# Retention and two MLPs on one core: Strassen in both products from the second MLP's first block on

## The chip, the cores and the metric

The kernel runs on one core of one Trainium2 chip. The metric is the device time of one execution in microseconds (us), lower is better. The profile splits a core into TensorE (PE, with its weight loads PEld), VectorE (DVE), ScalarE (ACT), GpSimd (POOL) and SyncE (SP); the last two only issue DMAs here.

## The reference, cut to what matters

```python
for t in range(S):                      # B, H, S, D = 4, 8, 768, 64
    state = gamma * state + k[t] (x) v[t]
    y[t] = scale * q[t] @ state
x = y as (B * S, H * D)                 # 3072 tokens x 512
h = x @ w_in;  x = max(0.01 * h, h) @ w_out          # first layer, 512 -> 2048 -> 512
h = max(x @ moe2_w_in, 0);  out = (h * h) @ moe2_w_out   # second layer, same sizes
```

Everything is float32, and the weights reach the chip as float64 words.

## The kernel before

**Blocks.** The 3072 tokens are cut into NB = 3 blocks of TB = 1024 tokens (c = one third of the sequence, for all four batches). A layer runs block by block, first layer first. A float32 product is made of three float32r matmuls, high*high, low*high, high*low (`product` line 470, `emit_out` line 577), so each operand is split into a rounded part (a copy on ACT) and a remainder (a subtraction on DVE).

**Two ways to multiply.** The "in" product of a block (1024 tokens, 512 to 2048) is plain in the first block of the first layer (`emit_plain`, line 535: 384 matmuls of 512 columns) and by Strassen's seven products elsewhere (`emit_in`, line 495: 8 steps q of 42 matmuls, 336). The "out" product (2048 to 512) is plain in the first layer and in block 0 of the second (`emit_out`: 16 parts j, two halves of 512 tokens, 12 matmuls each, 384). Blocks 1 and 2 of the second layer go through `both_block` (line 697), which has Strassen in both: a first stretch with `first_half` and `second_half` (336 matmuls), then seven stages over `STAGES` with the weight combinations of `read_stage` (336 matmuls).

**Weights.** `cast` (line 292) turns a staged tile of 128 x 1024 float64 words into float32: two activations on ACT (L296, L297), a shift, a bit merge and an addition on DVE (L298, L299, L302). `make_in` (line 334) adds and splits the seven combinations of an in-weight and stores them in `wid`; `make_out` (line 372) splits an out-weight and stores it in `wou`. First-layer weights are cast in block 0 (`plain_in`, `make_out`), and combined in block 1 (`make_in`, through `wraw`). Five of the eight second-layer in-weights (`AHEAD`) are cast and combined beside block 2 of the first layer; the other three, and all eight out-weights, in block 0 of the second. `out_combinations` (line 388) makes the four sums of an out-weight that Strassen needs: q = 0, 1 at the end of block 0, q = 2 to 7 beside the first stretch of block 1 (lines 713 to 723).

**Attention.** One pair of heads of one batch and one block is a unit `up`. `load_pair` brings q, k and v; `prep_pair` (line 143) scales q and v on DVE (L148, L154); `scores` (line 172) multiplies k by q into two PSUM banks `sc`, for blocks 1 and 2 both from `ps_h` (three banks, tag "h", which also hold `pa`, `pd`, `pb` of the in product), and masks them on DVE (L193); `values` (line 207) fills bank `y`. `score_next` (line 247) preps and scores one pair in the middle of each step q, `values` follows at the end of the step. Block 0's attention runs before everything (lines 791 to 801), block 1's and block 2's beside the blocks ahead of them.

**Order.** `pin` (line 101) fixes the order on PE, on SP (`load`) and on POOL (`store`) to that of the program text. ACT and DVE are ordered when the program is built, by readiness; `tc.issue_after(mark[0])`, `(mark[1])` puts a helper's ACT and DVE work behind the split marked last (`split_g`, `split_rot`). SP holds all loads, POOL all stores but the last two. Every engine takes its instructions in that order: an instruction that waits holds up those behind it.

Of the kernel before, what the change touches and what calls it, by code (L numbers as in the profile page):

```python
# [9 lines left out]
F32 = mybir.dt.float32  # L10
# [32 lines left out]
AHEAD = {0: 0, 1: 1, 3: 2, 5: 4, 6: 6}  # L43
# [7 lines left out]
def retention_then_two_mlps(  # L51
# [47 lines left out]
    behind = {}  # L99

# [27 lines left out]
    def load_pair(up):  # L128
# [9 lines left out]
        t = [a_p.tile([P, T], F32, tag=f"r{i}", name="r", bufs=2 + i) for i in range(2)]  # L138
# [4 lines left out]
    def prep_pair(up):  # L143
# [3 lines left out]
        qs = a_p.tile([P, 2, P], F32, tag="qs", name="qs", bufs=1)  # L147
# [24 lines left out]
    def scores(up):  # L172
# [67 lines left out]
    n_load, n_prep, n_done = [0], [0], [0]  # L240
# [6 lines left out]
    def score_next(last):  # L247
        n = n_prep[0]
        if n < last:
            loads_to(n + 1)  # L250
            prep_pair(ups[n])
            scores(ups[n])
            n_prep[0] += 1

    def value_to(n):
        while n_done[0] < n:
            values(ups[n_done[0]])
            n_done[0] += 1
            loads_to(n_done[0] + 2)

    def attend(last):

        n = n_prep[0]
        score_next(last)
        value_to(min(n, last))
        loads_to(min(n_done[0] + 3, n_prep[0] + 2))
# [4 lines left out]
    wraw = {}  # L271
# [4 lines left out]
    for q in range(NQ):  # L276
        wraw[q] = dram.tile([P, 1024], F32, name=f"wraw{q}")
    wou = [dram.tile([P, 8 if lay else 4, NQ, 2, 256], F32, name=f"wou{lay}") for lay in range(2)]
    for b in range(NB):
        ydr[b] = dram.tile([P, KB, TB], F32, name=f"ydr{b}")  # L280
    src = (w1, w2)
    stage, n_stage = {}, [0]

    def load_w(lay, q, half):
        if (lay, q, half) in stage:
            return
        n_stage[0] += 1
        pool, bufs = (late["p"], 1) if late and n_stage[0] % 3 == 0 else (w_p, 2)
        t = stage[lay, q, half] = pool.tile([P, 1024], U64, tag="sg", name="sg", bufs=bufs)
        load(out=t, in_=src[lay][q, half])  # L290
# [34 lines left out]
    def plain_in(q):  # L325
        load_w(0, q, 0)
        f = w_p.tile([P, 4, 256], F32, tag="wf", name="wf", bufs=1)
        cast(stage.pop((0, q, 0)), f.rearrange("p n c -> p (n c)"))
# [5 lines left out]
    def make_in(lay, b, q, ahead=False):  # L334
        f = w_p.tile([P, 7, 256], F32, tag="wf", name="wf", bufs=1)
        mid = f[:, 1:5].rearrange("p n c -> p (n c)")
        if lay == 0:
            load(out=mid, in_=wraw[q])
        else:
            load_w(lay, q, 0)  # L340
            cast(stage.pop((lay, q, 0)), mid)
        nc.vector.tensor_tensor(out=f[:, 0], in0=f[:, 3], in1=f[:, 4], op=ALU.subtract)
        nc.vector.tensor_tensor(out=f[:, 4], in0=f[:, 4], in1=f[:, 1], op=ALU.add)
        nc.vector.tensor_tensor(out=f[:, 5], in0=f[:, 1], in1=f[:, 0], op=ALU.subtract)
        nc.vector.tensor_tensor(out=f[:, 6], in0=f[:, 2], in1=f[:, 5], op=ALU.subtract)
        if ahead:
            a = late["p"].tile([P, 2, 4, 256], F32R, tag="ea", name="ea")
            c = late["p"].tile([P, 2, 3, 256], F32R, tag="eb", name="eb")
        else:
            a, c = in_tiles(lay, b, q)  # L350
        pair_up(a, f[:, 3:7])
        pair_up(c, f[:, 0:3])
        store(out=wid[lay, q][:, 0:2048], in_=a.rearrange("p l n c -> p (l n c)").bitcast(F32))
        store(out=wid[lay, q][:, 2048:3584], in_=c.rearrange("p l n c -> p (l n c)").bitcast(F32))
        if not ahead:
            put_in(lay, q, a, c)
# [7 lines left out]
    def get_in(lay, b, q):  # L364
        if lay == 0 and b == 0:
            plain_in(q)
        elif (lay == 0 and b == 1) or (lay == 1 and b == 0 and q not in AHEAD.values()):
            make_in(lay, b, q)
        else:
            read_in(lay, b, q)  # L370

    def make_out(lay, q):
        load_w(lay, q, 1)
        if lay == 0 and 0 < q < NQ - 1:
            f = g_p.tile([P, 2, T], F32, tag=f"t{NQ - 1}", name="of", bufs=1).rearrange("p j c -> p (j c)")
        elif lay and q:
            f = late["p"].tile([P, 1024], F32, tag=("ea", "eb")[q % 2], name="of")
        else:
            f = w_p.tile([P, 1024], F32, tag="wf", name="of", bufs=1)
        cast(stage.pop((lay, q, 1)), f)  # L380
        o = o_p.tile([P, 4, 2, 256], F32R, tag="wo", name="wo", bufs=2)
        pair_up(o.rearrange("p n l c -> p l n c"), f.rearrange("p (n c) -> p n c", n=4))
        put_units(lay, q, 0, o)
        wout[lay, q] = o
        if lay:
            store(out=wraw[q], in_=f)

    def out_combinations(q, f, ta, tb):
        load(out=f, in_=wraw[q])
# [7 lines left out]
        for n, t in ((0, ta), (2, tb)):  # L397
            u = t.bitcast(F32R).rearrange("p (n l c) -> p n l c", n=2, l=2)
            h = f[:, n * 256:(n + 2) * 256].rearrange("p (n c) -> p n c", n=2)
            nc.scalar.copy(u[:, :, 0], h)  # L400
            nc.vector.tensor_tensor(out=u[:, :, 1], in0=h, in1=u[:, :, 0].bitcast(F32), op=ALU.subtract)
            store(
                out=wou[1][:, 4 + n:6 + n, q].rearrange("p n l c -> p n (l c)"),
                in_=t.rearrange("p (n c) -> p n c", n=2),
            )
# [8 lines left out]
    def put_units(lay, q, n, t):  # L414
        store(
            out=wou[lay][:, n:n + 4, q].rearrange("p n l c -> p n (l c)"),
            in_=t.bitcast(F32).rearrange("p n l c -> p n (l c)"),
        )

    def read_out(lay, q, spare=None):  # L420
        if spare:
            o = spare[0].tile([P, 4, 2, 256], F32R, tag=spare[1], name="wo", bufs=spare[2])
        else:
            o = o_p.tile([P, 4, 2, 256], F32R, tag="wo", name="wo", bufs=2)
        load(
            out=o.bitcast(F32).rearrange("p n l c -> p n (l c)"),
            in_=wou[lay][:, 0:4, q].rearrange("p n l c -> p n (l c)"),
        )
        wout[lay, q] = o
# [56 lines left out]
    def act_sbuf(lay, g, on_act):  # L486
        if lay == 0:
            nc.scalar.activation(out=g, in_=g, func=AF.Lrelu)  # L488
        elif on_act:
# [5 lines left out]
    def emit_in(lay, b, q):  # L495
# [13 lines left out]
        nc.vector.tensor_tensor(out=c12, in0=c12, in1=pd, op=ALU.add)  # L509
        act_sbuf(lay, c12, True)  # L510
        yield
        product(lay, b, q, 7, pa, False, True)
        nc.vector.tensor_tensor(out=c22, in0=c22, in1=pa, op=ALU.add)  # L513
        act_sbuf(lay, c22, True)
# [4 lines left out]
        act_sbuf(lay, c11, False)  # L519
# [3 lines left out]
        if lay == 0:  # L523
            nc.scalar.activation(out=g, in_=pa, func=AF.Lrelu)
        else:
            nc.scalar.activation(out=g, in_=pa, func=AF.Relu)
# [470 lines left out]
```

## Time and profile before

| | us |
|---|---|
| median of 3 runs | 1148.55 (1140.07, 1148.55, 1153.57) |
| the profiled execution | 1139.64 |
| its span, first to last instruction | 1137.9 |
| attention of block 0 and first products | 0 to 60.5 |
| first layer: block 0 / 1 / 2 | to 272.1 / 488.4 / 654.1 |
| second layer: block 0 / 1 / 2 | to 823.2 / 979.3 / 1134.1 |

The stage limits are the times at which PE takes up the first `pa` product of the next block in the timeline. Matmuls overlap in the records, so a row's mean of 395 ns is not the pitch; the pitch is a stage's time over its matmuls.

### The profile page before, as it was taken

To read this page: it belongs to the slowest core of one execution; us is meant where nothing else is said; L and a number is where in the kernel's file an instruction comes from. 1 tells how busy PE (TensorE), PEld (TensorE's weight loads), DVE (VectorE), ACT (ScalarE), POOL (GpSimd) and SP (SyncE) were. 2 spreads that over 40 slices of the span, in tenths; PEclk is the share of its full clock that TensorE was granted. 3 is DMA by queue.
4 is the path that set the end of the run, shared out by engine and by line. 5 is a ranking of instruction groups with operands and counts; after the bars stand their busy time and mean duration, and the time that the engine had idled before them with its cause. 6 is when DMAs were issued, how large, how long until landed. Compare 5 with 4: busy or idle time off the path is not lost.

```text
span 1137.9 us, 14882 instructions
## 1 busy us (share of the span) xinstructions
PE 1109.4 (97%) x5690; PEld 879.7 (77%) x5690; DVE 678.1 (60%) x1082; ACT 541.9 (48%) x847; POOL 74.7 (7%) x130
## 2 busy tenths in 40 slices
PE   7899999999999999999999999999999999999998
PEld 5567777777777777788888887788787888888886
DVE  6856564555453535544467567777357877555853
ACT  3635453323433333344455366665256655455542
POOL 0000000001000000010001010111101000000000
PEclk9999999999999999999999999999999999999999
DMA  9556563666556555479788878957869967257571
GB/s 362 222 190 236 204 240 121 225 197 217 186 200 209 200 188 184 158 291 355 265 316 313 325 268 323 389 210 244 305 242 361 366 209 300 87 192 249 192 241 56
DMA packets 75015, 274.14 MB, mean 241 GB/s; under 512 B 6976, under 2 KB 9536, under 8 KB 64704
## 3 DMA queue, kind: packets, MB, share of 16 engines
q1 hardware_dynamic: 57120, 197.81, 49.0%
q0 software_dynamic: 17248, 74.98, 17.2%
q8 instruction: 45, 0.74, 0.3%
q10 hardware_dynamic: 576, 0.40, 0.1%
q14 instruction: 26, 0.21, 0.1%
HBM read 197.66 MB, written 75.50 MB: 240 GB/s over the span
## 4 chain that ended last, share of the span: by engine, by line
PE 86%; DMA 7%; DVE 4%; ACT 2%; issue 1%; ACTq 0%; SPq 0%; DVEq 0%
PE acc L113 41%; PE pa L113 25%; PE pd L113 8%; PE pb L113 5%; DMA wf<-wraw 4%; PE y L113 4%; PE sc L113 3%; DMA wo<-wou 1%; DMA wa<-wid 1%; DMA qt<-qtab 1%; ACT sg L297 1%; ACT wa L322 1%; DVE pm L193 0%; ACT of L296 0%; DVE g L509 0%
## 5 line engine op out<-in xcount | busy, mean ns | idle before, releaser
L113 PE MATMUL acc<-gh,wo 128*128 128x512 f32 x800 | 211.1, 395 | 1.2 <-DMA wo<-wou 1.2
L113 PE MATMUL pa<-xh,wa 128*128 128x512 f32 x576 | 182.6, 398 | 6.3 <-ACT g L483 2.2
L113 PEld LDWEIGHTS acc<-gh,wo 128*128 128x128 f32 x800 | 148.9, 188 | 37.1 <-issue 2.4
L113 PE MATMUL acc<-rot,wu 128*128 128x512 f32 x672 | 157.1, 395 | 0.0
L113 PEld LDWEIGHTS acc<-rot,wu 128*128 128x128 f32 x672 | 126.1, 188 | 30.6
L113 PEld LDWEIGHTS pa<-xh,wa 128*128 128x128 f32 x576 | 106.4, 188 | 33.2 <-ACT g L483 2.6
L113 PE MATMUL pa<-xl,wa 128*128 128x512 f32 x288 | 113.4, 394 | 1.5 <-DVE xl L439 1.5
L113 PE MATMUL acc<-gl,wo 128*128 128x512 f32 x400 | 113.6, 391 | 0.0
L113 PE MATMUL pd<-xh,wa 128*128 128x512 f32 x320 | 99.9, 394 | 0.9 <-ACT g L483 0.9
L113 PE MATMUL pa<-xh,wb 128*128 128x512 f32 x320 | 100.2, 394 | 0.0
L574 DVE TENSOR_TENSOR gl<-g,gh 128x512 fp32r<-128x512 f32 x100 | 67.7, 688 | 49.9 <-PE acc L113 29.5
L113 PEld LDWEIGHTS acc<-gl,wo 128*128 128x128 f32 x400 | 75.1, 188 | 16.6
L113 PE MATMUL acc<-gg,wo 128*128 128x512 f32 x336 | 83.7, 398 | 0.0
L573 ACT CAST gh<-g 128x512 fp32r<-128x512 f32 x100 | 60.5, 619 | 43.6 <-PE acc L113 43.3
L113 PEld LDWEIGHTS acc<-gg,wo 128*128 128x128 f32 x336 | 62.6, 188 | 15.6 <-issue 1.4
L113 PEld LDWEIGHTS pd<-xh,wa 128*128 128x128 f32 x320 | 60.4, 190 | 15.2 <-ACT g L483 2.2
L639 DVE TENSOR_TENSOR rot<-gu,rot 128x512 fp32r<-128x512 f32 x80 | 54.7, 688 | 26.8 <-ACT rot L638 26.5
L113 PEld LDWEIGHTS pa<-xh,wb 128*128 128x128 f32 x320 | 59.2, 188 | 13.7 <-DVE g L513 0.6
L638 ACT CAST rot<-gu 128x512 fp32r<-128x512 f32 x80 | 49.7, 621 | 42.2 <-PE acc L113 36.6
L488 ACT ACTIVATE g<-g 128x512 f32<-128x512 f32 x48 | 30.3, 632 | 82.1 <-DVE g L513 36.0
L113 PEld LDWEIGHTS pa<-xl,wa 128*128 128x128 f32 x288 | 54.3, 189 | 13.5 <-DVE xl L439 1.9
L113 PE MATMUL pd<-xl,wa 128*128 128x512 f32 x160 | 62.7, 392 | 0.0
(117 smaller groups left out, 1573.4 us busy)
## 6 DMA issues: line engine op xcount, KB each, us to landing
wo<-wou SPq DMA_DIRECT2D x40, 1024.0 KB, 7.2
sg<-w SPq DMA_DIRECT2D x32, 1024.0 KB, 8.7
wa<-wid SPq DMA_DIRECT2D x29, 1024.0 KB, 8.6
wu<-wou SPq DMA_DIRECT2D x56, 512.0 KB, 5.2
wb<-wid SPq DMA_DIRECT2D x29, 768.0 KB, 7.0
wou<-wo POOLq DMA_DIRECT2D x16, 1024.0 KB, 5.6
r<-first SPq DMA_DIRECT2D x48, 256.0 KB, 3.5
wid<-wa POOLq DMA_DIRECT2D x11, 1024.0 KB, 4.3
```

The costliest lines, as they stand in the source:

```text
L113: pin(nc.tensor.matmul(**kw))
L297: nc.scalar.activation(out=lo, in_=lo, func=AF.Copy, scale=2.0 ** -29)
L322: nc.scalar.copy(t[:, 0], s)
L488: nc.scalar.activation(out=g, in_=g, func=AF.Lrelu)
L573: mark[0] = nc.scalar.copy(gh, g).ins
L574: mark[1] = nc.vector.tensor_tensor(out=gl, in0=g, in1=gh.bitcast(F32), op=ALU.subtract).ins
L638: mark[0] = nc.scalar.copy(r[:, 0], s).ins
L639: mark[1] = nc.vector.tensor_tensor(out=r[:, 1], in0=s, in1=r[:, 0].bitcast(F32), op=ALU.subtract).ins
```

## The change

Block 0 of the second layer goes through `both_block` as well. Its weights are made earlier. `SOON` lists 12 of the 16 second-layer weights (all in-weights, out-weights q = 4 to 7); each is cast in three pieces of 384, 384 and 256 columns, 20 pieces beside block 0 of the first layer and 16 beside block 1, and stored as plain float32 in `wflt`. The combinations of in-weights `FIRST` (2, 3, 5, 7) are made in eight halves beside block 1 (`make_half`), those of 0 and 1 in SBUF at the end of block 2, those of 4 and 6 inside `both_block(0)` (`units_here`). `make_units` makes all eight units of an out-weight: q = 0 to 3 (`HERE`, cast there from float64) and q = 4 beside block 2, q = 5 to 7 in `both_block(0)`. All these loads are issued by `store`, on POOL's queue. In block 1 of the first layer `make_in` stands earlier in the step. Separately, `prep_pair` runs one pair ahead of `scores`, and in the middle of a step the second `sc` bank is `y` of `ps_a`. `both_block(1)` has no weights to make any more.

```diff
+FIRST = (2, 3, 5, 7)
+HERE = (0, 1, 2, 3)
+SOON = [(q, 0) for q in FIRST + (0, 1, 4, 6)] + [(q, 1) for q in range(NQ) if q not in HERE]
...
-        late["p"] = mid.enter_context(tc.tile_pool(name="late", bufs=1))
+        late["p"] = mid.enter_context(tc.tile_pool(name="late", bufs=1, reuse_waits="tile"))
...
+    @contextmanager
+    def aside():
+        with tc.issue_after(mark[0]), tc.issue_after(mark[1]):
+            yield
...
-        t = [a_p.tile([P, T], F32, tag=f"r{i}", name="r", bufs=2 + i) for i in range(2)]
+        t = [a_p.tile([P, T], F32, tag=f"r{i}", name="r", bufs=3) for i in range(2)]
...
-            sc = [ps_h.tile([P, 512], F32, tag="h", name="sc") for h in range(2)]
+            other = (ps_a, "y") if alone else (ps_h, "h")
+            sc = [p.tile([P, 512], F32, tag=t, name="sc") for p, t in ((ps_h, "h"), other)]
...
+    def prep_to(n):
+        while n_prep[0] < min(n, len(ups)):
+            loads_to(n_prep[0] + 1)
+            prep_pair(ups[n_prep[0]])
+            n_prep[0] += 1
...
+        if last:
+            prep_to(min(n_score[0] + 1, last))
...
+    def load_piece(n):
+        if n < 3 * len(SOON):
+            q, half, c = piece(n)
+            t = stage[n] = a_p.tile([P, 384], U64, tag=f"m{4 - n % 2}", name="st", bufs=1)
+            store(out=t[:, :c.stop - c.start], in_=w2[q, half][:, c])
+
+    def cast_piece(n):
+        q, half, c = piece(n)
+        f = a_p.tile([P, 384], F32, tag="sf", name="sf", bufs=2)[:, :c.stop - c.start]
+        cast(stage.pop(n)[:, :c.stop - c.start], f)
+        store(out=wflt[q, half][:, c], in_=f)
...
+    def combine(f, a, c, x=None):
+        tt = nc.vector.tensor_tensor
+        here = x is None
+        if here:
+            split_low(c, 1, 3, f[:, 2:4])
+            x = f[:, 1:4]
+        split_low(a, 0, 1, f[:, 0:1])
+        tt(out=f[:, 0], in0=f[:, 0], in1=f[:, 1], op=ALU.subtract)
+        tt(out=x[:, 0], in0=f[:, 1], in1=f[:, 2], op=ALU.add)
+        tt(out=x[:, 1], in0=f[:, 2], in1=f[:, 0], op=ALU.subtract)
+        tt(out=x[:, 2], in0=f[:, 3], in1=x[:, 1], op=ALU.subtract)
+        if here:
+            yield
+        split_low(a, 1, 4, x[:, 0:3])
+        if not here:
+            yield
+            split_low(c, 1, 3, f[:, 2:4])
+        split_low(c, 0, 1, f[:, 0:1])
...
+    def make_units(q, f, *to):
+        if q in HERE:
+            t = late["p"].tile([P, 1024], U64, tag="sg", name="sg")
+            store(out=t, in_=w2[q, 1])
+            yield
+            cast(t, f)
+        else:
+            store(out=f, in_=wflt[q, 1])
+        yield
+        h = [f[:, n * 512:n * 512 + 512].rearrange("p (n c) -> p n c", n=2) for n in range(2)]
+        for n in range(2):
+            out_units(q, 2 * n, h[n], to[n])
         yield
...
-            if b == 1:
+            if b == 0 and n < NQ - 1 and n != 5:
...
+                if n in (0, 2, 4):
+                    made = make_units(5 + n // 2, *v[:5])
                     next(made)
+                    if n == 0:
+                        here = [units_here(4, v[5], v[7]), units_here(6, v[6], v[5])]
...
+    def side(n):
+        if n_piece[0] < 3 * len(SOON):
+            next_piece()
+            if n < NQ:
+                next_piece()
...
+        elif n % 2:
+            next_half()
...
+                if b == 1:
+                    side(2 * q)
+                elif 0 < q < 6 and q - 1 in HERE:
+                    with aside():
+                        next(made)
...
+            elif nl and 0 < q < 6:
+                with aside():
+                    next(made)
+                    next(made, None)
+                if q < 5:
+                    made = units_ahead(q)
...
+    for b in range(NB):
+        both_block(b)
```

## Rows read from the trace of the kernel before

**Rows 1.** The page, part 1: busy time and share of the span by engine.

```profile
span 1137.9 us, 14882 instructions
PE 1109.4 (97%) x5690; PEld 879.7 (77%) x5690; DVE 678.1 (60%) x1082; ACT 541.9 (48%) x847; POOL 74.7 (7%) x130
```

**Rows 2.** Busy time by stretch: limits, length, each engine's busy time, clock, DMA.

```profile
core 0: us, PE busy (x) PEld busy (x) DVE busy (x) ACT busy (x) POOL busy (x), PEclk, DMA share, GB/s
0.00:60.50 60.50, 48.05 (x496) 33.75 (x496) 45.52 (x104) 28.23 (x53) 2.15 (x7) 0.97 0.72 274
60.50:200.10 139.60, 137.54 (x760) 107.60 (x760) 78.47 (x116) 68.14 (x90) 9.84 (x15) 0.99 0.56 204
...
272.10:417.00 144.90, 138.11 (x718) 106.33 (x716) 64.52 (x120) 55.82 (x93) 9.06 (x17) 0.99 0.57 202
...
488.40:654.10 165.70, 165.70 (x721) 135.08 (x720) 90.78 (x120) 81.58 (x123) 10.94 (x21) 1.00 0.83 312
654.10:823.20 169.10, 166.97 (x722) 134.64 (x721) 117.56 (x154) 99.97 (x145) 19.50 (x33) 1.00 0.79 290
823.20:979.30 156.10, 154.84 (x673) 125.96 (x672) 113.90 (x182) 87.77 (x147) 13.79 (x22) 1.00 0.75 278
979.30:1134.10 154.80, 154.79 (x673) 125.95 (x671) 88.02 (x135) 74.61 (x127) 3.79 (x7) 1.00 0.53 180
823.20:901.10 77.90, 76.64 (x338) 63.05 (x337) 53.77 (x97) 46.66 (x83) 9.97 (x15) 1.00 0.84 310
979.30:1055.70 76.40, 76.40 (x338) 63.24 (x337) 40.01 (x61) 39.88 (x70) 0.54 (x1) 1.00 0.59 202
277.40:281.90 4.50, 4.50 (x12) 3.27 (x12) 1.93 (x2) 1.99 (x3) 1.07 (x2) 0.62 0.79 316
```

**Rows 3.** Waits of PE: us in total, times, longest.

```profile
PE sc L113 <- DVE g L509: 4.6, 6, 1.4
...
PE sc L113 <- DVE vs L154: 3.1, 5, 1.1
...
PE pa L113 <- ACT g L483: 2.2, 1, 2.2
...
PE pa L113 <- DMA wa<-wid: 1.3, 1, 1.3
```

**Rows 4.** DVE's groups by shape: count, busy us, mean ns, idle before.

```profile
L299 DVE SCALAR_TENSOR_TENSOR wf<-sg,wf 128x1024 uint32<-128x1024 uint32 x16 | 19.5, 1219 | 0.2
...
L298 DVE TENSOR_SCALAR wf<-wf 128x1024 uint32<-128x1024 uint32 x16 | 11.3, 704 | 15.2 <-ACT wf L296 14.9
...
L401 DVE TENSOR_TENSOR of<-of 128x512 fp32r<-128x512 f32 x16 | 10.9, 684 | 1.5 <-ACT of L400 1.5
...
L343 DVE TENSOR_TENSOR wf<-wf 128x256 f32<-128x256 f32 x16 | 6.8, 426 | 0.6
...
L148 DVE TENSOR_TENSOR qs<-r,qt 128x128 f32<-128x128 f32 x16 | 4.6, 284 | 1.7 <-DMA qt<-qtab 1.4 <-PE y L113 0.2
```

**Rows 5.** ACT's groups by shape, the same columns.

```profile
L483 ACT COPY g<-pa 128x512 f32<-128x512 f32 x48 | 28.2, 587 | 40.4 <-PE pa L113 40.4
...
L296 ACT ACTIVATE wf<-sg 128x1024 f32<-128x1024 f32 x16 | 18.2, 1138 | 4.7 <-DMA sg<-w 4.7
L232 ACT COPY xs<-y 128x256 f32<-128x256 f32 x48 | 17.8, 371 | 41.5 <-PE y L113 41.4
```

**Rows 6.** ACT's waits for staged weights: the same in 0 to 270 and overall.

```profile
ACT sg L297 <- DMA sg<-w: 5.6, 5, 2.2
...
ACT wf L296 <- DMA sg<-w: 4.7, 1, 4.7
...
ACT of L296 <- DMA sg<-w: 3.1, 2, 2.0
```

**Rows 7.** DMA issues: queue, count, size, median us from issue to landing.

```profile
sg<-w SPq DMA_DIRECT2D x32, 1024.0 KB, 8.7
...
wou<-wo POOLq DMA_DIRECT2D x16, 1024.0 KB, 5.6
```

**Rows 8.** POOL's issue instructions of line 119: ns min/median/max.

```profile
L119 POOL DMA_DIRECT2D wraw<-wf x8: 554/554/942, 27.5 to 171.1; - x8
```

More of the change, by code (lines that the diff above doesn't have):

```diff
@@ L170, in increment, with scores @@
             )
-    def scores(up):
+    def scores(up, alone):
         u, p = up
@@ L280, in retention_then_two_mlps, with load_w, piece @@
         ydr[b] = dram.tile([P, KB, TB], F32, name=f"ydr{b}")
[L281 to L290, printed above, removed]
+    stage = {}
+    def load_w(q, half):
+        t = stage[q, half] = w_p.tile([P, 1024], U64, tag="sg", name="sg", bufs=2)
+        load(out=t, in_=w1[q, half])
+    def piece(n):
+        k, part = divmod(n, 3)
+        return *SOON[k], slice(384 * part, min(384 * part + 384, 1024))
+    def load_piece(n):
[8 more added lines that the diff above has]
+        store(out=wflt[q, half][:, c], in_=f)
     def cast(s, r):
@@ L332, in plain_in @@
         win[0, q] = a
[L334 to L356, printed above, removed]
@@ new lines, in blocks, with put_wid, make_in @@
+    def blocks(q, half=None):
+        t = wflt[q, 0].rearrange("p (n c) -> p n c", n=4)
+        return t if half is None else t[:, :, half * P:half * P + P]
+    def put_wid(lay, q, t, half=slice(None)):
+        o, m = (0, 8) if t.shape[2] == 4 else (2048, 6)
+        store(
+            out=wid[lay, q][:, o:o + m * 256].rearrange("p (n c) -> p n c", n=m)[:, :, half],
+            in_=t.rearrange("p l n c -> p (l n) c").bitcast(F32),
+        )
+    def make_in(b, q):
+        f = w_p.tile([P, 4, 256], F32, tag="wf", name="wf", bufs=1)
+        load(out=f.rearrange("p n c -> p (n c)"), in_=wraw[q])
+        a, c = in_tiles(0, b, q)
+        for _ in combine(f, a, c):
+            pass
+        put_wid(0, q, a)
+        put_wid(0, q, c)
+        put_in(0, q, a, c)
@@ new lines, in load_half, with make_half @@
+    def load_half(n):
+        if n < 2 * len(FIRST):
+            f = stage[-1, n] = a_p.tile([P, 4, P], F32, tag="sf", name="wf", bufs=2)
+            store(out=f, in_=blocks(FIRST[n // 2], n % 2))
+    def make_half(n):
+        a = a_p.tile([P, 2, 4, P], F32R, tag="m4", name="ma", bufs=1)
+        c = a_p.tile([P, 2, 3, P], F32R, tag="m3", name="mc", bufs=1)
+        f = stage.pop((-1, n))
+        half = slice(n % 2 * P, n % 2 * P + P)
+        for _ in combine(f, a, c):
+            pass
+        put_wid(1, FIRST[n // 2], a, half)
+        put_wid(1, FIRST[n // 2], c, half)
@@ L396, in out_combinations @@
         tt(out=a12, in0=a12, in1=a22, op=ALU.subtract)
[L397 to L405, printed above, removed]
+        for n in range(2):
+            out_units(q, 4 + 2 * n, h[n], to[2 + n])
     def scratch(*tags):
@@ L623, in read_units, with units_here @@
         put_in(1, q, a, c)
+    def units_here(q, f, *x):
+        store(out=f, in_=wflt[q, 0])
+        yield
+        f, *x = (v.rearrange("p (n c) -> p n c", n=4) for v in (f, *x))
+        a, c = unit_tiles()
+        put_in(1, q, a, c)
+        steps = combine(f, a, c, *x)
+        next(steps)
+        if x:
+            put_wid(1, q, a)
+        yield
+        next(steps, None)
+        if not x:
+            put_wid(1, q, a)
+        put_wid(1, q, c)
     def read_stage(n, ks):
@@ L806, in read_x, with put_out, next_piece, next_half @@
         load(out=xs[NB + b], in_=ydr[b])
-    def put_out(lay, b, j, part=(0, 12)):
-        emit_out(lay, b, 0, j, part, j == 0, j == NJ - 1)
+    def put_out(b, j, part=(0, 12)):
+        emit_out(0, b, 0, j, part, j == 0, j == NJ - 1)
+    n_piece, n_half = [0], [0]
+    def next_piece():
+        n = n_piece[0]
+        if n == 0:
+            load_piece(0)
+            load_piece(1)
+        with aside():
+            cast_piece(n)
+        load_piece(n + 2)
+        n_piece[0] += 1
+    def side(n):
[3 more added lines that the diff above has]
+                next_piece()
+            if n_piece[0] == 3 * len(SOON):
+                load_half(0)
+                load_half(1)
+        elif n % 2:
+            next_half()
+    def next_half():
+        with aside():
+            make_half(n_half[0])
+        load_half(n_half[0] + 2)
+        n_half[0] += 1
+    def units_ahead(q):
+        f = late["p"].tile([P, 1024], F32, tag="of", name="of", bufs=2)
+        to = [w_p.tile([P, 2, 1024], F32, tag="sg", name="of", bufs=2) for _ in range(2)]
+        g = make_units(q, f, *(t[:, n] for t in to for n in range(2)))
+        next(g)
+        return g
     def split_late(i):
@@ L936 @@
+    swap_right()
+    for b in range(NB):
+        both_block(b)
 _OUT = ((NB, P, KB, TB), "float32")
```

401 lines of the change are left out of this document (197 added, 204 removed).

## The prediction

> **What bounds the kernel now.** I read the page's busy shares first [rows 1]: PE is busy 1109.4 of 1137.9 us, DVE 60%, ACT 48%. So PE sets the time, and a change pays by taking matmuls away, by closing the 28.5 us in which PE stands, or not at all. The second view is busy time by stretch, cut where PE takes up a new block [rows 2]. The reader is to see two things there. First, block 2 of the second layer is 672 matmuls in 154.8 us with PE busy all of it: 0.2304 us each. Block 2 of the first layer has 720 in 165.7, 0.2301 each, also without a stop. That is the pitch of a covered PE. Block 0 of the second layer has 720 in 169.1; at the pitch that is 165.9, so 3.2 us are stops. Second, the large gaps are elsewhere: 12.4 us in the first 60.5, 2.1 in 60.5 to 200.1, 6.8 in 272.1 to 417. The third view, PE's waits, names them [rows 3]: scores behind DVE's addition L509 (4.6 us, six times), scores behind the scaled v (3.1 us, five times), one product behind ACT's copy (2.2 us).
>
> One stop is dearer than its wait. After that copy, 12 matmuls took 4.5 us at a granted clock of 0.62 [rows 2], so mostly at 1.2 instead of 2.4 GHz, against 2.8 us at the pitch. A stop of 2.2 us costs 3.9.
>
> **The change part by part.**
>
> *Second layer, block 0.* The out product falls from 384 to 336 matmuls, 48 x 0.2304 = 11.1 us. What the block then looks like is seen in block 1 of before, which also makes weights beside its first stretch: 156.1 us, 1.3 above block 2, its one wait being for `wa` from `wid` [rows 2, 3]. The side work on DVE, which is the fuller engine: a `make_units` is 2 x 0.684 for the plain units and 4 x 0.426 + 2 x 0.684 for the sums [rows 4], 1.37 + 3.07; three make 13.3. A `units_here` is splits of 256, 768, 512 and 256 columns (0.43 + 0.95 + 0.68 + 0.43, the 768 set between 512 and 1024) and four sums of 256, 4.19; two make 8.4. Together 21.7 us; block 1 of before had six sums of 3.07, 18.4. Block 2, without side work, has DVE busy 40.0 in 76.4 of its first stretch [rows 2], 5.0 per step of 9.55. Step 3 now gets 3.08 (first part of `units_here`) and 1.37: 9.45 of 9.55; step 4 gets 1.11 + 3.07: 9.18. DVE is full for two steps. I charge 1.0 us for that, so 157.1 instead of 169.1: **-12.0**. Bounds: 154.8 (-14.3) if all is covered, and 154.8 + 21.7 = 176.5 (+7.4) if PE waited for every side instruction.
>
> *Second layer, block 1.* Its six sums go away: 156.1 becomes the 154.8 of block 2, **-1.3** (0 to -1.3).
>
> *Second score bank.* In a step `pa` and `pd` hold two of three `ps_h` banks, so the second `sc` waits until L509 has added `pd`. With `y`, free since the last step's `values`, it does not: **-4.6** (0 to -4.6) [rows 3]. Late next is the mask on DVE, needed only for `values` at the end of the step.
>
> *Scaled q and v ahead.* It can take away the 3.1 us of waits for v, all in the first 60 us. But DVE is busy 45.5 of 60.5 there [rows 2] and does the same work; order alone changes. I take half, **-1.5** (0 to -3.1). The third `r` buffer and the second `qs` cost nothing but space; their loads are the same, issued earlier on SP, where none of the waits on PE comes from.
>
> *Pieces and halves beside the first layer.* A 384-column piece on DVE: shift 0.30 (an estimate, 384/1024 of 0.704 and a start), merge and addition 0.55 each, between 0.426 and 0.684 [rows 4]: 1.41. A 256 one: 0.25 + 2 x 0.43 = 1.10. On ACT 2 x 0.48 and 2 x 0.37, between 0.371 and 0.587 [rows 5]. Two of three are 384 wide, so a mean of 1.31 and 0.89. A half of `make_half`: four sums of 128 columns at 0.284 and splits of 256, 128, 384 and 128: 2.69 on DVE, some 1.35 on ACT. In 60.5 to 200.1 fifteen pieces lift DVE from 78.5 to 98 and ACT from 68 to 82 of 139.6; in 272.1 to 417 sixteen pieces and four halves lift DVE from 64.5 to 96 and ACT from 56 to 75 of 144.9 [rows 2]. That is 70% at most, no more than block 0 of the second layer carried (117.6 of 169.1) with PE busy 99%. Bytes: in the first layer's block 1 a third of 16 weights' 1.5 MB and eight halves of 1.1 MB are 17 MB in 216 us, 82 GB/s on top of 202; 312 GB/s were moved in block 2 without a stop of PE [rows 2]. So capacity hides it all. What may show is order. A cast's first instruction on ACT waits for its load, and behind it stand the copies that free PE's banks. Slack for such a copy: after product 1, PE has product 5 (6 matmuls) and an out part (12), 4.2 us, less the copy's 0.59 [rows 5]: 3.6 us. ACT waited for staged weights up to 4.7 us before [rows 6]. The pieces' loads go to POOL's queue, behind stores that wait for DVE, and in block 1's first four steps two casts stand together twice, so that the next two loads have about 9 us to land; a 1 MB transfer takes 5.6 to 8.7 [rows 7], the pieces being smaller. I charge one stop of the size above: **+3.9**. Bounds: 0, and eight such stops, one for each of those doubles, 31.2.
>
> *Block 2 of the first layer.* Out go five in-weights made ahead (cast 3.14, four sums 1.70, splits 1.22 + 0.95: 7.0 of DVE each), in come four out-weights of cast, eight units and sums (3.14 + 4 x 0.684 + 1.70 = 7.6) and one without cast (4.4): 34.8 for 35.0. In the last stretch two `units_here` add 8.4. The four cast weights are loaded by POOL behind the four stores of the weight before. If each were as late as 4.7 us, PE would see 4.7 - 3.6 = 1.1 of it, 4.4 in all; I take **+1.0** (0 to 4.4).
>
> The moved `make_in` issues the same loads in the same order on SP (wf, r, wo, step after step), and the finer pool release comes where PE has no stop; both at 0, with the bounds of the pieces around them, since they share ACT's order.
>
> Sum: -12.0 - 1.3 - 4.6 - 1.5 + 3.9 + 1.0 = **-14.5**. The profiled execution took 1139.64, so it would take 1125.1. The runs' median is 1148.55, 8.9 above; from it the sum gives 1134.1. A new measurement can fall on either level, so I take the middle, **1129.6**.
>
> *A rule against it.* The issue of a DMA by POOL took 0.55 us, at most 0.94 [rows 8], in a span in which DVE ran 32 shifts of 0.70 us: no issue was held up by as much as one shift. The Trainium skill (SBUF — State Buffer, "Who interferes with whom") says that a DMA issued from GpSimd can seem held up by a DVE operation, because GpSimd is kept from writing its descriptors. By that rule each of the some 56 loads moved from SP to POOL would start up to a shift later; two pieces ahead that moves no term, and it would only make the slower rival below likelier. The trace does not bear it out, and I leave that rival low.
>
> **The rivals.**
>
> *Given back beside the work.* Two more stops of 3.9 in the first layer, and a tenth of the 21.7 us showing in block 0 beyond the 1.0: -14.5 + 7.8 + 2.2 = -4.5, **1140**. For it: DVE is full in two steps, ACT has waited for weights. Against it: block 1 of before lost 1.3 in the same position.
>
> *Late pieces, slower.* In block 1 of the first layer, steps 0 to 3, each pair of casts stops ACT longer than the slack of 3.6 us, from where PE stands and its clock falls: eight stops, 31.2 instead of 3.9, so 1129.6 + 27.3 = **1157**. For it: POOL's queue is in order and holds stores that wait for DVE. Against it: only two casts between load and use need be late for nothing to show, and ACT never waited for a weight after the first layer's block 0 [rows 6].
>
> *Everything covered.* All lower ends: -14.3 - 1.3 - 4.6 - 3.1 = -23.3, **1121**. For it: two blocks of 165.7 and 154.8 without a stop. Against it: the full DVE steps.
>
> *The attention edits do nothing* (DVE is the one that is late): -14.5 + 6.1 = -8.4, 1136; this lies within the forecast's own range, 1121 to 1138.
>
> **How the numbers follow.** Forecast 0.55, given back 0.25, late pieces 0.07, everything covered 0.13. A measurement of this kernel can tell about 1%, 11.5 us, from no change. Faster by more: most of the forecast (0.50), the covered case and a little of the first rival, 0.65. Within: 0.05 and most of "given back", 0.27. Slower: 0.08. The range runs from 1113 (all lower ends from the profiled execution, 1116, and 3 us for the stop at 277 going too) to 1148 (given back, counted from the median: 1144, and one more stop).
>
> **What would show it.** Right: the page has 5642 matmuls; the second layer's three blocks take about 157, 155 and 155 us; no wait of scores behind L509's successor; DVE over 90% in steps 3 and 4 of the new block. Wrong: waits of PE behind ACT's copies with ACT waiting for a DMA of a piece, a granted clock well below 1 in 272 to 420, or a first stretch of the new block over 85 us.

## The result and the profile after

The changed kernel takes 1151.14 us (median of 20 runs, 1148.1 to 1163.49), the kernel before 1144.41 beside it (20 runs): a ratio of 1.006 [1.0033, 1.0087], so slower by 0.6%. The forecast was 1129.6, a gain, and 1151.14 lies outside its range too. Medians are of all runs; ratios leave out the few that were over 1.5% slower than their kernel's fastest, all at a lower granted clock. The profiled execution took 1154.02. The page's first part:

```profile
span 1152.3 us, 15363 instructions
PE 1112.5 (97%) x5642; PEld 879.0 (76%) x5642; DVE 723.8 (63%) x1285; ACT 567.3 (49%) x978; POOL 136.8 (12%) x230
```

48 matmuls fewer than [rows 1], as written, yet PE is busy 3 us longer. Busy time by stretch, cut as [rows 2] (the first limit is where the first out product starts), shows where:

```profile
0.00:87.70 87.70, 68.48 (x550) 48.64 (x551) 57.32 (x119) 36.55 (x62) 3.02 (x9) 0.79 0.68 249
87.70:299.40 211.70, 205.92 (x1190) 159.72 (x1189) 132.17 (x244) 98.82 (x159) 34.57 (x62) 0.97 0.66 229
299.40:516.30 216.90, 207.05 (x1169) 157.66 (x1168) 137.33 (x315) 102.51 (x208) 47.83 (x77) 1.00 0.78 266
516.30:683.70 167.40, 166.41 (x721) 134.93 (x721) 91.07 (x139) 82.71 (x136) 24.56 (x40) 1.00 0.84 309
683.70:838.90 155.20, 155.20 (x673) 125.99 (x672) 117.08 (x186) 91.09 (x155) 18.74 (x31) 1.00 0.76 280
838.90:993.50 154.60, 154.60 (x673) 126.14 (x672) 100.13 (x146) 81.05 (x134) 4.32 (x8) 1.00 0.61 218
993.50:1148.20 154.70, 154.70 (x673) 125.96 (x671) 88.02 (x135) 74.60 (x127) 3.78 (x7) 1.00 0.53 180
```

The first rows of the kernel before, cut at the same places (71.1, and 272.3 where [rows 2] has 272.1):

```profile
0.00:71.10 71.10, 57.56 (x551) 40.82 (x552) 49.77 (x112) 31.20 (x57) 2.87 (x8) 0.95 0.73 273
71.10:272.30 201.20, 200.23 (x1189) 156.13 (x1188) 114.89 (x188) 88.04 (x122) 12.01 (x20) 1.00 0.55 197
272.30:488.40 216.10, 209.31 (x1169) 161.10 (x1168) 102.51 (x190) 78.71 (x130) 11.77 (x23) 0.99 0.57 198
```

The second layer did what was forecast: block 0 fell from 169.1 to 155.2, block 1 from 156.1 to 154.6, with PE busy all of both. That is 15.5 us won. The first layer lost more: the stretch ahead of its out products grew from 71.1 to 87.7, block 0 from 201.2 to 211.7, block 1 from 216.1 to 216.9, block 2 from 165.7 to 167.4, together 29.6. Only 14.5 of the 29.6 are stops of PE. The other 15.1 are a longer busy time for the same matmuls; the largest parts are 10.9 at the start, where the mean clock was 0.79 against 0.95, and 5.7 in block 0, at 0.97 against 1.00. DVE was busy 63% of block 1 and ACT 47%: neither is full. PE's waits name other places than [rows 3]:

```profile
PE y L121 <- DVE state L243: 8.7, 6, 5.2
PE pa L121 <- ACT g L563: 4.6, 2, 2.7
PE sc L121 <- DMA r<-first: 3.9, 1, 3.9
PE pa L121 <- ACT wa L353: 3.6, 1, 3.6
PE pa L121 <- DVE g L591: 2.6, 3, 1.6
PE sc L121 <- DVE vs L162: 2.6, 7, 0.6
```

The scores' wait for the addition to `pd` is gone, and four new stops have come. Three were followed back in the timeline. The first, 5.2 us: ACT, in order of time (start, length, line, in brackets the idle time before it):

```profile
57.10 0.62 ACT L647 CAST gh<-g 128x512 fp32r<-128x512 f32 x1
61.78 1.10 ACT L328 ACTIVATE sg<-sg 128x1024 uint32<-128x1024 uint32 x1 [4.06 <-DMA sg<-w]
62.78 0.19 ACT L209 COPY s<-sc 128x64 f32<-128x64 f32 x1
62.87 0.37 ACT L241 COPY xs<-y 128x256 f32<-128x256 f32 x1
```

The cast of the next weight tile stands ahead of two short copies that attention needs, and its load, issued at 55.83, is not there. ACT stands 4.06 us, the copies behind it are late, DVE's state and PE's `y` with them. Another wait of ACT for a weight tile, 3.7 us up to 76.6, comes ahead of the two stops for `wa` (3.6 and 1.9 us).

The second, 3.9 us at 243: SP stood from 181 to 215.75 ahead of one load. `wf` has one buffer; the store that empties it was far back on POOL, and after it the last out-weight was cast and split in the same buffer. SP first, then POOL:

```profile
181.12 0.33 SPq L124 DMA_DIRECT2D r<-first  x1
215.75 0.33 SPq L124 DMA_DIRECT2D wf<-wraw  x1
...
232.82 7.88 SPq L124 DMA_DIRECT2D r<-first  x4
```

```profile
202.60 0.54 POOL L127 DMA_DIRECT2D wflt<-sf  x1 [10.47 <-DVE sf L333]
...
203.91 0.54 POOL L127 DMA_DIRECT2D wraw<-wf  x1 [0.24 <-issue]
```

POOL waits 10.5 us for a piece's conversion with that store behind it, and SP's `r` loads stand behind `wf`. That this stand alone made the stop is not shown: the load that PE waits for was issued at 232.82, after SP had stood another 11.3 us for PE to release a `wo` tile, and it landed 14.4 us later, with the DMA engines busy without a break at the end (last section). The third, 2.7 us at 432, on ACT:

```profile
425.57 1.13 ACT L647 CAST gh<-g 128x512 fp32r<-128x512 f32 x2
433.12 0.40 ACT L366 CAST mc<-wf 128x256 fp32r<-128x256 f32 x1 [6.42 <-DMA wid<-mc]
...
433.63 0.36 ACT L241 COPY xs<-y 128x256 f32<-128x256 f32 x1
433.89 0.59 ACT L563 COPY g<-pa 128x512 f32<-128x512 f32 x1
```

ACT waits 6.4 us for the store of the half before, which must leave the one `mc` buffer, and the copy that frees PE's bank comes after. All three are of one kind: an in-order engine stands for a transfer, and behind it stands work for PE.

### The profile page after: what moved, and what is told of

Same layout as the page of the kernel before. It is cut to its first block, busy times and chain, and to the rows that moved or that the text cites. A ratio compares the mean times of both kernels' runs of the same rounds, so it can differ in the third digit from the quotient of the medians.

```text
span 1152.3 us, 15363 instructions
## 1 busy us (share of the span) xinstructions
PE 1112.5 (97%) x5642; PEld 879.0 (76%) x5642; DVE 723.8 (63%) x1285; ACT 567.3 (49%) x978; POOL 136.8 (12%) x230
## 4 chain that ended last, share of the span: by engine, by line
PE 67%; issue 13%; DMA 10%; DVE 5%; POOL 3%; ACT 1%; SPq 0%; ACTq 0%; POOLq 0%; DVEq 0%
PE acc L121 32%; PE pa L121 20%; PE pd L121 7%; DMA r<-first 3%; PE pb L121 3%; PE y L121 3%; PE sc L121 2%; DMA wf<-wraw 2%; DMA of<-wflt 1%; DMA st<-w 1%; DMA sg<-w 1%; POOL wou L127 1%; DMA wid<-mc 1%; POOL wflt L127 1%; DMA qt<-qtab 1%
## 5 line engine op out<-in xcount | busy, mean ns | idle before, releaser
L121 PE MATMUL acc<-rot,wu 128*128 128x512 f32 x1008 | 235.7, 395 | 0.0
L121 PEld LDWEIGHTS acc<-rot,wu 128*128 128x128 f32 x1008 | 189.2, 188 | 46.0
L121 PE MATMUL acc<-gh,wo 128*128 128x512 f32 x600 | 161.0, 400 | 2.3 <-ACT gh L647 2.0
L121 PEld LDWEIGHTS acc<-gh,wo 128*128 128x128 f32 x600 | 112.8, 190 | 31.0 <-ACT gh L647 3.2
L731 DVE TENSOR_TENSOR rot<-gu,rot 128x512 fp32r<-128x512 f32 x120 | 82.0, 688 | 38.1 <-ACT rot L730 37.6
L730 ACT CAST rot<-gu 128x512 fp32r<-128x512 f32 x120 | 74.5, 621 | 61.7 <-PE acc L121 54.4
L121 PE MATMUL acc<-gl,wo 128*128 128x512 f32 x300 | 85.5, 392 | 0.0
L121 PEld LDWEIGHTS acc<-gl,wo 128*128 128x128 f32 x300 | 56.7, 189 | 12.8
L121 PE MATMUL acc<-gg,wo 128*128 128x512 f32 x252 | 62.9, 398 | 0.0
L121 PE MATMUL pa<-xl,wb 128*128 128x512 f32 x160 | 62.5, 390 | 0.0
```

What stands on the lines that cost most here:

```text
L121: pin(nc.tensor.matmul(**kw))
L730: mark[0] = nc.scalar.copy(r[:, 0], s).ins
L731: mark[1] = nc.vector.tensor_tensor(out=r[:, 1], in0=s, in1=r[:, 0].bitcast(F32), op=ALU.subtract).ins
```

## The experiments

All runs were timed in five rounds beside the kernel before. Ratios are to it, with 95% intervals, and runs of different rounds are compared by them.

| run | us | ratio |
|---|---|---|
| b_prep | 1166.64 | 1.018 [1.0121, 1.0239] |
| b_prep_r2 | 1145.88 | 1.0018 [0.9984, 1.0052] |
| b_bank | 1131.93 | 0.9897 [0.9855, 0.9939] |
| a_noprep | 1143.03 | 1.0008 [0.997, 1.0046] |
| a_noatt | 1163.31 | 1.0164 [1.0117, 1.0211] |
| a_nocast | 1151.43 | 1.0036 [0.9994, 1.0078] |
| a_get | 1144.05 | 0.9991 [0.9958, 1.0023] |
| a_store | 1149.68 | 1.0023 [0.9986, 1.0061] |
| a_early | 1148.52 | 0.999 [0.9946, 1.0034] |
| a_st3 | 1139.79 | 0.9977 [0.994, 1.0015] |
| a_dve | 1142.45 | 0.9974 [0.9931, 1.0018] |
| a_earlyst3 | 1143.3 | 1.0008 [0.997, 1.0046] |
| t_traffic | 1160.4 | 1.0127 [1.0075, 1.018] |
| t_act | 1156.52 | 1.0114 [1.0069, 1.016] |
| t_free | 1143.37 | 1.0017 [0.9991, 1.0043] |
| b_bank2 | 1131.75 | 0.9899 [0.9854, 0.9944] |
| a_st3dve | 1132.3 | 0.9897 [0.985, 0.9944] |
| a_three | 1130.21 | 0.9871 [0.983, 0.9912] |

### The change taken apart

**b_prep** and **b_bank**: the kernel before with the scaled q and v one pair ahead (and its third `r` buffer) alone, and with the second score bank alone.

> The kernel before with the scaling of q and v one pair ahead (and its third r buffer) as the only edit. Theory (the edit frees SP's queue on paper, so ACT is given casts of block 0's weights before their loads can land, and stands with the copies behind them): 8 to 16 us slower than before, a wait of y behind the state update of over 4 us near 60 us of the span and a wait of pa behind wa near 80. Rival (the pieces and their POOL queue cost the time): 0 to 3 us faster than before, no such waits. Rival (the low clock from 27 to 44 us was chance): as before within 2 us, in the middle of its runs.

> The kernel before with y as the second score bank as the only edit. All theories of the loss leave this part alone: the six waits of scores behind the addition L509 go, 4.6 us faster (ratio 0.996); if the wait comes back behind another release, no difference.

**a_noprep** and **a_noatt**: the changed kernel without the first of these edits, and without both.

> The changed kernel with scaling one pair ahead undone (two r0 buffers, one qs), second score bank kept. Theory (scaling ahead costs the start): 12 to 18 us faster than the changed kernel, some 8 us faster than before (ratio 0.991 to 0.995), first out matmul of the first block back from 88 to about 72 us. Rival (pieces): no faster than the changed kernel by more than 3 us.

> The changed kernel with both attention edits undone. Theory: about 4 us above the same kernel with the bank kept, so 4 to 5 us faster than before (ratio 0.995 to 0.998); the waits of scores behind the addition of pd come back, SP's stand of some 27 us behind the store of wraw near 190 to 216 us stays, since the pieces on POOL cause it. Rival (pieces): slower than before by 5 us or more.

By the ratios the pair ahead costs some 21 us alone and some 6 in the changed kernel (intervals that just overlap): more than b_prep's theory had, and between a_noprep's theory and its rival. The bank is worth 11 to 12 us alone, more than the 4.6 of its waits: in the profiled executions PE stands 5.4 us less and is busy 4.5 us less. In the changed kernel it is worth 18 to 20 (1163.3 to 1143.0). With neither, the re-staged weights are 20 us slower than before, although they win 15 in the second layer, so they cost some 35. That fell against the theory, which had a_noatt faster than before; its waits show the missing bank:

```profile
PE sc L121 <- DVE g L585: 14.5, 7, 5.4
```

[rows 3] had 4.6 us in six such waits. In b_bank the two stretches (limits as above) are 0.9 and 6.8 us shorter than before, at the same work:

```profile
69.30:269.60 200.30, 200.30 (x1190) 156.21 (x1190) 115.02 (x188) 87.02 (x121) 12.17 (x20) 1.00 0.56 199
269.60:478.90 209.30, 205.56 (x1170) 158.37 (x1169) 102.02 (x190) 78.87 (x130) 11.81 (x23) 1.00 0.60 204
```

Against these, the changed kernel's 211.7 and 216.9 are 19 us of loss.

### Why the pair ahead costs

**b_prep_r2**: b_prep with the buffers of `r` as before.

```diff
-        t = [a_p.tile([P, T], F32, tag=f"r{i}", name="r", bufs=3) for i in range(2)]
+        t = [a_p.tile([P, T], F32, tag=f"r{i}", name="r", bufs=2 + i) for i in range(2)]
```

> The kernel before with the scaled q and v made one pair ahead, as in the run with that edit alone, but with the buffers of r as they were (two for q and k, three for v). Theory: the 23 us that the edit cost come from the third buffer of q and k, which lets the loads of the weight tiles move ahead on SP and with them their casts on ScalarE, in front of the copies that the attention waits for; with two buffers those casts go back and the time falls to 1140 to 1148 us, with no stop of y behind the state above 3 us before the first out product. Rival: making q and v ahead is itself what costs (two VectorE operations put in front of others); then it stays at 1158 to 1168 us.

The theory held: 1145.9. PE's waits of b_prep, then of b_prep_r2:

```profile
PE y L113 <- DVE state L234: 6.8, 3, 5.2
...
PE pa L113 <- ACT wa L329: 2.7, 1, 2.7
```

```profile
PE y L113 <- DVE state L234: 4.0, 5, 1.1
```

The 5.2 us stop belongs to the one extra buffer of q and k. In the order of the built programs it is the cast's second activation on ACT that b_prep has in front of the copies of the state and of `xs` and b_prep_r2 behind them. All 847 ACT instructions of b_prep_r2 follow each other as in the kernel before; in b_prep 17 stand elsewhere. How much of the 21 us the order costs is less sure. The profiled executions differ by 21.4 us, and 15.0 of these are PE's busy time (1129.9 against 1114.9): b_prep's ran at a clock of 0.50 from 16 to 48 us, b_prep_r2's at 1.00. Executions with a mean clock of 0.990 or 0.991 took 1156.94 in b_prep and 1143.3 to 1148.52 in b_prep_r2, 8 to 14 us apart.

### What of the re-staged weights costs

Four single edits on a_noprep. **a_nocast** keeps one ACT operation of each piece's conversion and leaves out the other four, so its second-layer weights are not the right ones; **a_get** puts block 1's `make_in` back at the end of the step; **a_store** issues the plain weights' stores from ACT; **a_early** loads the next `wf` right behind the combination before it.

```diff
-        cast(stage.pop(n)[:, :c.stop - c.start], f)
+        nc.scalar.activation(out=f, in_=..., func=AF.Copy, scale=2.0 ** -112)
```

```diff
-        store(out=wraw[q], in_=f.rearrange("p n c -> p (n c)"))
+        pin(nc.scalar.dma_start(out=wraw[q], in_=f.rearrange("p n c -> p (n c)")))
```

```diff
         put_in(0, q, a, c)
+        if q + 1 < NQ:
+            load_in(q + 1)
```

> The changed kernel without the work one pair ahead; of each of the 42 pieces' five operations of conversion one on ScalarE is kept, one on ScalarE and three on VectorE are left out, so the second layer's weights are not those of the reference; all loads and stores of the pieces stay. Theory A: the pieces cost by the work that they put on VectorE and ScalarE in front of evacuations (about 1.9 us each, 80 us in all); blocks 0 to 2 of the first layer get 8 to 14 us shorter, 1129 to 1135 us. Theory B: they cost by their transfers (buffers that wait for stores, landings that are late); then no more than 4 us is won, 1139 to 1144 us.

> The changed kernel without the work one pair ahead, with the combinations of block 1's weights back at the end of the step, where the kernel before has them. Theory: the place costs nothing, as the prediction said, and the time stays within 3 us of 1143. Rival 1: the earlier place puts its 4 us of VectorE and ScalarE work in front of evacuations, and block 1 gets 5 to 10 us shorter (1133 to 1138 us). Rival 2: it was needed with the pieces in between, and the time rises by 5 us or more.

> The changed kernel without the work one pair ahead, with the eight stores of the plain weights issued by ScalarE right behind its copy, no longer by GpSimd behind the stores of the pieces. Theory: one store that sat behind a piece's held SP and the r loads up and cost block 0 of the first layer 4 to 6 us; 1136 to 1140 us against 1143 of the kernel without this edit. Rival: the rows behind SP were idle time that nothing needed; 1141 to 1145 us.

> The changed kernel without the work one pair ahead; in block 1 the load of the next plain weight (wf<-wraw) is issued right behind the combination of the one before, no longer behind the loads of wo and r on SP. Theory: ScalarE, which now opens each combination with a copy of the loaded tile, stands for that load (14.9 us in the changed kernel's block 1, three of its five stops of TensorE come right behind such a wait); with the load earlier these waits fall below 4 us, block 1 gets 5 to 8 us shorter, 1135 to 1139 us. Rival: TensorE then stops for the next late landing (pieces, halves) and nothing is won: 1141 to 1146 us.

None won anything (the text on record says 42 pieces; the changed kernel has 36). With four of five operations left out the time is no lower, so nothing here points at the engines' work on the pieces. In a_early SP's `r` loads stood behind the earlier `wf` load, and scores waited 5.65 us for one of them. In the timelines of block 1 of a_noprep and these four, every stop of PE of a microsecond or more but one has, in the 8 us ahead of it, ACT or DVE standing for a transfer: `wf`, `st`, `r`, or a store that has to leave `ma` or `mc`. Taken alone this proves little, as some four fifths of these blocks lie within 8 us of such a wait. Nor are these edits of one thing: against a_noprep, 53 to 64 of the 978 ACT instructions and 74 to 146 of the 1285 on DVE stand elsewhere in the built order of a_get, a_store and a_early. No gain from the place of `make_in` was seen (a_get).

**a_st3** stages the pieces in three tiles, three ahead; **a_dve** has VectorE make the two copies that open `make_in`'s combination; **a_earlyst3** joins a_st3 and a_early.

```diff
-            t = stage[n] = a_p.tile([P, 384], U64, tag=f"m{4 - n % 2}", name="st", bufs=1)
+            t = stage[n] = a_p.tile([P, 384], U64, tag=f"m{4 - n % 3}", name="st", bufs=1)
...
-        for _ in combine(f, a, c):
+        for _ in combine(f, a, c, copy=nc.vector.tensor_copy):
```

> The changed kernel without the work one pair ahead; the pieces of the second layer's weights are staged in three tiles and loaded three ahead, no longer two. Theory: ScalarE's waits for st<-w (14.9 us from block 0 to block 1 in the changed kernel) go, and with them one or two stops of TensorE of 1.7 to 3.3 us in each block; 1137 to 1141 us. Rival: as with the third buffer of r, the built order moves the conversions up as far as the buffers let them, ScalarE stands as long in other places; 1142 to 1152 us.

> The changed kernel without the work one pair ahead; in block 1's combinations the two copies that open them are made by VectorE, no longer by ScalarE, so that VectorE waits for the load as in the kernel before. Theory: TensorE waits sooner for ScalarE, whose copies free its banks, than for VectorE; block 1 loses its stops behind wf<-wraw and is 4 to 7 us shorter, 1136 to 1140 us. Rival: VectorE's waits stop TensorE as much; 1141 to 1147 us.

> The changed kernel without the work one pair ahead, with both the earlier load of wf and three staging tiles for the pieces. Theory that the landings are what costs: 1130 to 1136 us, as the first layer then keeps near the 575 us that it takes with the second score bank alone, and the second layer its gain of 15 us. Rival (the built order follows the buffers): not better than the better of the two edits, 1137 to 1150 us.

The gains of the single edits are too small to tell from none. Joined with the early load the third tile won nothing: scores stood 5.78 us for `r` again.

### The transfers alone

On b_bank, whose second layer makes its own weights: **t_traffic** adds the pieces' loads and stores at the changed kernel's places, into spare tensors; **t_act** adds one ACT copy on each; **t_free** is t_traffic with each store reading a tile of zeros, so that POOL waits for no load. b_bank2 is their base.

```diff
-        store(out=wcopy[k][:, c], in_=t[:, :w])
+        store(out=wcopy[k][:, c], in_=full[:, :w])
```

> The kernel before with the second score bank, and beside its first layer the transfers of the pieces and halves of the changed kernel without any work of an engine on them: 42 piece loads and stores and 8 half loads and stores on GpSimd's queue into spare tensors, at the changed kernel's places (the second layer stays as in the kernel before). Theory A, transfers on a busy chip stretch the other landings: 1137 to 1144 us against 1132 of the kernel with the bank alone. Theory B, it is ScalarE's and VectorE's standing for the landings that costs: 1130 to 1136 us.

> The same, with one ScalarE copy on each piece and each half as it lands (0.55 us each, 50 of them, in the order that the changed kernel writes them). Theory B: ScalarE stands for landings and PE behind it, 1137 to 1146 us, at least 4 us above the run with the transfers alone. Theory A: no more than 2 us above it.

> The kernel with the transfers alone, changed so that no store waits for a load: the stores of pieces and halves take their bytes from a tile of zeros that is ready from the start, so that GpSimd's queue issues without standing for a landing; the number, the size and the places of the transfers stay. Theory A1, the bytes on the transfer engines cost by stretching the other landings: 1148 to 1160 us as with the transfers alone (1160.4). Theory A2, what costs is that GpSimd's one queue stands for each landing and the stores of the weights behind it go out late, which holds SP and its r loads: 1131 to 1139 us. Between 1139 and 1148 us both have a part.

> The kernel before with the second score bank alone once more, beside the runs above on the same chip: 1130 to 1135 us.

As written, these kernels came to 41 loads and 39 stores of pieces and to no halves, less than the texts say: some 21 MB (28 x 384 + 13 x 256 KB of loads, 26 x 192 + 13 x 128 KB of stores). Even so t_traffic is by the ratios some 26 us slower than b_bank2, more than either theory had, with no engine operation added. An ACT copy on each piece adds no time, though PE then stands behind ACT's copies (17.5 us) instead of for `r` (8.9). In t_free, with most of POOL's waits gone, some 13 of the 26 are left, and PE no longer stands for `r`. POOL's waits for its own piece transfers from 67.9 to 504.9 us, the first two blocks of t_traffic (t_traffic, then t_free):

```profile
POOL st L119 <- DMA wcopy<-st: 220.4, 39, 13.8
```

```profile
POOL st L119 <- DMA st<-w: 59.1, 13, 10.1
```

While POOL stands, the stores of finished weights stand behind it, and SP stands for them; in block 1 of t_traffic:

```profile
SPq L116 <- DMA wid<-wa: 31.1, 1, 31.1
```

The bytes show in the landings (last column: median us from issue to landing, in the same window; b_bank2, then t_free):

```profile
r<-first SPq DMA_DIRECT2D x42, 256.0 KB, 3.2
wid<-wa POOLq DMA_DIRECT2D x8, 1024.0 KB, 4.2
...
wid<-wb POOLq DMA_DIRECT2D x8, 768.0 KB, 6.7
wf<-wraw SPq DMA_DIRECT2D x8, 512.0 KB, 7.6
```

```profile
r<-first SPq DMA_DIRECT2D x42, 256.0 KB, 4.4
wid<-wa POOLq DMA_DIRECT2D x8, 1024.0 KB, 7.1
...
wid<-wb POOLq DMA_DIRECT2D x8, 768.0 KB, 10.8
wf<-wraw SPq DMA_DIRECT2D x8, 512.0 KB, 10.0
```

These two groups of loads on SP's own queue land 1.2 and 2.4 us later, though a landing is counted from SP's own issue. SP's loads of `wo` (7.8, then 7.7 us) and `sg` (9.1, then 9.4) hardly do. The Trainium skill (DMA: Bandwidth & Descriptors, "Issuing engines are not separate DMA queues") says that transfers issued from different engines run on the same 16 DMA engines; the rows of `r` and `wf` agree.

That the 26 us are half POOL's queue and half bytes is not shown. The built order moved here too: against b_bank2, 36 of the 847 ACT instructions and 32 of the 1082 on DVE stand elsewhere in t_traffic, 17 and 40 in t_free, and in b_prep 17 were enough to lose time. And in the changed kernel POOL stands for something else than in t_traffic, above all for conversions of pieces on DVE (182.8 us in 27 waits in the first two blocks).

### A version that beats both

**a_st3dve** joins a_st3 and a_dve; **a_three** adds a_store's edit.

> The changed kernel without the work one pair ahead, with three staging tiles and with the opening copies of block 1's combinations on VectorE: the two edits that came out best. If they add, 1134 to 1138 us; if the waits move on to the next landing, 1138 to 1143 us. To beat both kernels and the second bank alone it would have to come below 1131 us.

> The changed kernel without the work one pair ahead, with three staging tiles, the opening copies of block 1's combinations on VectorE, and the plain weights' stores issued by ScalarE: in the run without the last edit SP stood 22 us for such a store behind GpSimd's queue, and a stop of 3.5 us behind the r loads came of it. If that is so, 1126 to 1130 us, below the second bank alone (1131.8); if the order that is built moves the stop elsewhere, 1131 to 1140 us.

Each edit alone was lost in the noise; two of them together win 1.1%. ACT's waits for these two transfers from 70 to 520 us, in a_noprep, then what is left of them in a_st3dve, where DVE waits for `wf`, as in the kernel before:

```profile
ACT sf L325 <- DMA st<-w: 18.1, 10, 4.0
...
ACT wb L364 <- DMA wf<-wraw: 14.3, 7, 3.5
```

```profile
ACT st L326 <- DMA st<-w: 3.5, 3, 1.9
...
DVE wb L364 <- DMA wf<-wraw: 12.0, 7, 3.0
```

The transfers and the arithmetic are the same, so some 12 of the 27 us that the re-staging costs (next section) come of ACT standing for landings, or of the order that was built with these edits. All three take a_noprep from 1143.0 to 1130.2, 1.3% below the kernel before and 1.8% below the changed one (1130.21 / 1151.14). Its lowest run is 1122.1, b_bank's 1129.2, but the medians of a_three and b_bank2 (1131.75) don't tell the two apart.

## Why the prediction was wrong

**Right: the second layer.** Block 0 was put at 157.1 and came at 155.2, block 1 at 154.8 and came at 154.6. The microsecond charged for full DVE steps was not paid: DVE was busy 8.97 of 9.5 us in step 3, 6.46 of 9.6 in step 4 and 9.36 of 9.5 in step 5 (steps 3 and 4 were named), with PE busy throughout.

**Wrong: "the third `r` buffer and the second `qs` cost nothing but space; their loads are the same, issued earlier on SP".** Taken as -1.5; by the ratios some +21 alone, +6 in the changed kernel. I looked for a wait of PE on SP, found none, and stopped there. Loads placed earlier on SP move the casts behind them forward on ACT, and that order is fixed for all executions. A part of the 21 is a low clock at the start, which other kernels had without this edit.

**Wrong in the path and in size: the pieces, +3.9, with block 2's +1.0.** By medians: before 1143.1, less 11.2 for the bank, less 15.5 for the second layer, makes 1116.4; a_noprep took 1143.0. So the re-staging costs some 27 us with the bank (35 without it). The argument from capacity held (no engine full) and said nothing: the charge was for one late load, by engines' shares. What the traces show of the cost lies in queues and landings: [rows 7] was used as the time of a transfer in a kernel that moves 42.8 MB in block 1, where the changed one moves 57.7, and "POOL's queue, behind stores that wait for DVE" was named without asking what else sits there. It held the stores that free `wf`, `ma`, `mc`. How the 27 divide between late landings, POOL's queue and the built order stays open; a_st3dve regains some 12 of them. The upper bound of 31.2 and the rival "late pieces" had the kind of stop (PE behind ACT, ACT standing for a transfer), but for loads of pieces in block 1. Only one stop of block 1 was of that sort, 1.7 us at 374 behind a 4.3 us wait for a piece. Its two stops behind ACT's copy followed waits for a plain weight (3.3 us) and for a half's store (6.4 us), and the larger losses stood ahead of block 0 and in it. That rival's 1157 was given 0.07; that it came closest to 1151 was partly luck.

**Wrong in size: the bank, -4.6.** The sum of its waits; it gave 11 to 12 alone and 18 to 20 where ACT and DVE run late. That it waited on "the addition of `pd`" was right.

**Sum of the terms as measured:** -15.5 - 11.2 + 27 + 6 = +6, against 6.7 measured (1151.14 - 1144.41). This has to come out near, as 27 is what was left over in a_noprep. Of the signs to look for, "waits of PE behind ACT's copies with ACT waiting for a DMA of a piece" came true in the one stop at 374, "a granted clock well below 1 in 272 to 420" did not (1.00 in block 1; the low clock came earlier, at the start and at 246), and the scores' wait is gone as said.

**The weighed rule** of the Trainium skill (SBUF — State Buffer, "Who interferes with whom"): POOL's 36 piece loads were issued in 543 ns at the median, 633 at most, beside a DVE that was busy 63% of the span. So by the issue times the rule is not borne out here; what delayed loads was the wait in front of them on POOL.

## What to carry to other kernels

Work moved beside a matmul stretch is not free because the engines have room: list which transfers it adds, on which in-order queue, and what stands behind each wait there, since one queue that stands for a landing holds every store and load after it. An extra buffer is an edit of the order, not only of space, and so was every other edit of loads and stores here: before an edit is read as a test of one thing, compare where each engine's instructions stand. Price a wait with the matmul clock after it, and test the parts of a change one by one; here the smallest, one score bank, was worth more than the whole.

## What the runs showed of the hardware

A stop's price differs from run to run. The copy at the start of the first layer's block 1 stopped PE for 2.2 us before, and 12 matmuls after it ran at a granted clock of 0.62 [rows 2]. In b_bank the stop is as long, but the clock stays (windows of 2 us, columns as [rows 2]):

```profile
272.00:274.00 2.00, 0.46 (x3) 0.03 (x1) 1.10 (x3) 0.68 (x1) 0.00 (x0) 1.00 0.94 218
274.00:276.00 2.00, 1.31 (x6) 1.05 (x6) 1.72 (x4) 2.00 (x4) 0.00 (x0) 1.00 0.97 347
276.00:278.00 2.00, 2.00 (x12) 1.29 (x12) 0.94 (x2) 0.70 (x2) 0.82 (x2) 1.00 0.65 258
```

In the changed kernel the 3.9 us stop at 243 was followed by some 10 us at 0.50, that is 1.2 instead of 2.4 GHz:

```profile
244.00:246.00 2.00, 0.00 (x0) 0.00 (x0) 0.00 (x0) 0.00 (x0) 0.54 (x1) 0.99 1.02 264
246.00:248.00 2.00, 0.74 (x2) 0.50 (x2) 0.69 (x3) 0.00 (x0) 0.00 (x0) 0.50 1.01 411
...
254.00:256.00 2.00, 2.00 (x6) 1.62 (x5) 1.70 (x5) 0.00 (x0) 0.00 (x0) 0.50 0.64 239
```

The clock was also 0.50 from 16 to 40 us or longer in the profiled executions of several of these kernels (b_prep, a_noprep and a_noatt among them, from 28 to 44 in the changed one), and 1.00 there in others (b_bank, a_early and a_store). In a_noprep (0.50) and a_early (1.00) ACT and DVE have the same order there, so the clock differed from execution to execution. That is part of the changed kernel's 87.7 us at the start, and those kernels' stage times at the start are not used.
